# Seven-product values in the second and third batch, casts on GpSimd, sums in pieces

## The chip, the cores and the metric

The kernel runs on one core of one Trainium2 chip. The metric is the device time of one execution in microseconds; of several runs the median is given. One execution is taken by the hardware profiler, and all views of the profile are of that one. The engines are called as in the profile: PE (TensorE, matmuls), PEld (its weight loads), DVE (VectorE), ACT (ScalarE), POOL (GpSimd) and SP (SyncE, which here issues DMAs in order).

## What is computed

Attention in which a query sees only the keys of its own cluster, then a gated feed-forward block over all tokens. There are 4 batches, 8 heads, 768 tokens and 64 columns per head; 16 centroids per head; d_model 512, d_ff 1536.

```python
q_assign = argmax(einsum('bhsd,hcd->bhsc', q_n, c_n))      # k_assign alike
mask = q_assign[:, :, :, None] == k_assign[:, :, None, :]
scores = where(mask, scale * q @ k.T, -1e9)
attn = exp(scores - max) / sum
x = (attn @ v) laid out as [3072, 512]
gate = 1 / (1 + exp(-(x @ w_gate)))
out = (gate * (x @ w_val)) @ w_out
```

## The kernel before

**Attention** runs as 384 steps, 96 for a batch. A step is one score matmul of 128 x 384 (L1066, tile sc), its exp on ACT (L1071, es) and, two steps later, three matmuls of the weights with the values (L1089, av). PE executes in program order, and so does every other engine, so the order in which the program issues instructions is the schedule.

**Preparation** of later heads is issued at given step numbers by `at(step, ...)`. For a pair of heads `pair_prep` (L1624) splits keys and queries into a high and a low half-precision part: a cast on DVE (L1631, tile hl) and a subtract on POOL (L1632), four of each for a pair. Then SP issues a DMA transpose (L412, tile T); the logits against the centroids (L436, lg) and the cluster pick on DVE (L451 to L471: lgs, mx, oh) follow. `v_cast` (L324, POOL) and `v_sum` (L332 to L339, DVE) prepare the values.

**Feed-forward.** The attention result of a batch is transposed into xTb. Its feed-forward work is put into a queue of atoms and is run during the next batch's 96 steps: each step adds a number of nanoseconds to a credit (ns20 to ns33 in the table of numbers, for quarters of a batch), and atoms are taken while it lasts. For a token half (blk, 384 tokens) and each of 12 column blocks (fc) of 128, `ffn_atoms` (L517) issues a gate group (4 matmuls 128 x 384, L532, and tanh on ACT, L538, tile th) and a value group (4 matmuls, L548, and one DVE instruction, L553, that forms (th + 1) * v into hT). The factor from the sigmoid in terms of tanh is folded elsewhere.

**Output.** `product_out` (L917) multiplies a pair of token blocks, or two pairs at once, by w_out in seven products (two 2x2 block matrices with seven half-size products in place of eight). It uses two PSUM banks, x and y, in turn; each product ends with an add on DVE into ob (L941) that frees its bank for the next but one. The operand sums come from `Sums.make` (L892, L909 to L915; 128 x 768). In the second and third batch the pair (0, 1) is done alone, its atoms alternating with gate and value groups of the second token half (`aside`); then (3, 2) and (4, 5) are done together.

The last batch has no attention behind it. `closing` does its gates and values in seven products too, over 2x2 blocks of (token half, pair of column blocks, half of the 512 rows). For this, `fin_weights` (L608) makes differences of weights and `fin_tokens` (L622) sums of tokens, on DVE.

**Buffers.** th has 3, the ring of PSUM banks for scores, gates and values 4, the output banks 2, hl 4, T 8, the raw keys and queries 3 each.

## Time and profile before

| | |
|---|---|
| Median of 3 runs | 319.14 us (319.08 to 319.54) |
| The profiled execution's own time | 319.12 us |
| Its span, first to last instruction | 317.3 us |
| Mean granted clock of PE | 1.00 |
| Matmuls and their weight loads | 3492 each |
| HBM traffic | 28.34 MB read, 6.29 MB written |

The span is what the profile's views cover; 1.8 us of the execution lie outside it. Busy times of PE overlap, since matmuls are pipelined: how long one holds the engine is seen in the distance from its start to the next start. A row of the timeline is start, duration, engine, line, operation, out<-in, partitions x columns and a count of joined instructions. A row of groups is line, engine, operation, tiles, shapes, count, busy us, mean ns of one, then idle time before and what ended it. A row of windows is the stretch, its length, and busy us (with counts) of PE, PEld, DVE, ACT and POOL, the clock, the DMA share and GB/s.

### The profile page before, as it was taken

Reading aid. Unit: us, or ns where it says so; the run is one execution under the profiler, and the core shown is the slowest. Engines: PE = TensorE matmul, PEld = TensorE weight load, DVE = VectorE, ACT = ScalarE, POOL = GpSimd, SP = SyncE. Lnnn points to the kernel's source line nnn. Section 1 sums busy time; section 2 is a strip of 40 time slices with the busy share of each in tenths; the row PEclk is TensorE's granted clock in tenths of the full one; section 3 lists DMA queues with packets and bytes.
Section 4 is the critical chain, followed back from the end, with each engine's and each line's share of the span. In section 5 each row is a group of like instructions: output and inputs, shape, how many; then the busy total and the mean of one; then the engine's idle time right before and its main releaser. Section 6 shows DMA issues by size and latency. Waiting matters only on the chain.

```text
span 317.3 us, 9228 instructions
## 1 busy us (share of the span) xinstructions
PE 310.0 (98%) x3492; PEld 218.8 (69%) x3492; DVE 238.6 (75%) x623; ACT 244.9 (77%) x555; POOL 120.9 (38%) x157
## 2 busy tenths in 40 slices
PE   7899999999999999999999999999999999999995
PEld 4688766766666666666777678766677678656685
DVE  5899756778688777686788688776888776678983
ACT  6688998797899887877776876777877887588621
POOL 5888454244434275423234333424212111026600
PEclk9999999999999999999999999999999999999999
DMA  7999998639848988976676455882506130300014
GB/s 196 379 259 169 271 164 143 176 83 264 242 100 163 204 221 136 199 217 161 106 193 153 151 118 134 248 153 53 112 2 76 55 27 14 145 1 3 0 35 165
DMA packets 77996, 45.16 MB, mean 142 GB/s; under 512 B 56896, under 2 KB 75520, under 8 KB 77952
## 3 DMA queue, kind: packets, MB, share of 16 engines
q1 hardware_dynamic: 73840, 39.66, 51.3%
q0 software_dynamic: 3680, 4.72, 9.1%
q8 instruction: 27, 0.44, 0.6%
q10 hardware_dynamic: 432, 0.20, 0.2%
q14 instruction: 17, 0.14, 0.1%
HBM read 28.34 MB, written 6.29 MB: 109 GB/s over the span
## 4 chain that ended last, share of the span: by engine, by line
PE 93%; DMA 2%; DVE 1%; POOL 1%; SPq 1%; issue 0%; ACT 0%; DVEq 0%
PE sc L1066 19%; PE g L532 15%; PE v L548 15%; PE av L1089 11%; PE o L994 9%; PE o L865 5%; PE lg L436 2%; PE o L699 2%; PE o_end L802 2%; PE av L699 2%; DMA kraw<-in_k_dram 2%; PE v L628 2%; PE y L699 2%; PE o L802 1%; PE av L802 1%; PE z L699 1%
## 5 line engine op out<-in xcount | busy, mean ns | idle before, releaser
L1071 ACT ACTIVATE es<-sc 128x384 f16<-128x384 f32 x384 | 174.1, 492 | 38.5 <-PE sc L1066 29.8
L1066 PE MATMUL sc<-T 128*128 128x384 f16 x384 | 117.3, 325 | 0.7 <-DVE T L1396 0.4
L1089 PEld LDWEIGHTS <-es 128*128 128x128 f16 x1152 | 81.3, 98 | 35.1 <-ACT es L1071 0.2
L1089 PE MATMUL av<-va,es 128*128 128x65 f16 x1152 | 97.6, 194 | 0.0
L553 DVE SCALAR_TENSOR_TENSOR hT<-th,v 128x384 f16<-128x384 f32 x72 | 39.8, 553 | 33.8 <-PE av L1089 29.6
L377 POOL TENSOR_TENSOR xp<-t,rec 128x384 f16<-128x384 f32 (+1 forms) x30 | 21.8, 726 | 97.3 <-DVE rec L374 49.2
L548 PE MATMUL v<-xTb,wv 128*128 128x384 f16 x288 | 58.5, 326 | 0.1
L532 PE MATMUL g<-xTb,wg 128*128 128x384 f16 x288 | 58.5, 326 | 0.0
L538 ACT ACTIVATE th<-g 128x384 f32<-128x384 f32 x72 | 35.4, 492 | 8.3 <-PE g L532 6.3
L1066 PEld LDWEIGHTS <-T 128*128 128x128 f16 x384 | 37.0, 96 | 1.2 <-DVE T L1396 0.7
L548 PEld LDWEIGHTS <-wv 128*128 128x128 f16 x288 | 28.0, 97 | 13.9 <-issue 0.3
L532 PEld LDWEIGHTS <-wg 128*128 128x128 f16 x288 | 27.9, 97 | 13.9
L1632 POOL TENSOR_TENSOR hl<-kraw,hl 128x384 f16<-128x384 f32 x22 | 20.2, 920 | 40.6 <-DVE hl L1631 25.9
L1632 POOL TENSOR_TENSOR hl<-qraw,hl 128x384 f16<-128x384 f32 x22 | 21.1, 961 | 11.1 <-DVE hl L1631 11.1
L865 PE MATMUL o<-wo,hT 128*128 128x512 f16 x72 | 19.9, 379 | 0.0
L372 DVE TENSOR_TENSOR t<-av,sv 128x390 f32<-128x390 f32 (+1 forms) x30 | 14.4, 480 | 7.1 <-PE av L1089 5.3
L941 DVE TENSOR_TENSOR ob<-o,ob 128x256 f32<-128x256 f32 (+1 forms) x28 | 15.0, 549 | 4.7 <-PE o L994 3.2
L708 POOL TENSOR_TENSOR hT<-T 128x384 f16<-128x384 f32 x12 | 11.8, 1001 | 16.2 <-DVE T L657 15.6
L994 PE MATMUL o<-wo,hT 128*128 128x256 f16 x108 | 16.8, 272 | 0.0
L994 PEld LDWEIGHTS <-sum 128*128 128x128 f16 x144 | 14.0, 97 | 3.3
L451 DVE TENSOR_REDUCE lgs<-lg 128x192 f32<-128x384 f32 x23 | 12.7, 551 | 3.0 <-PE lg L436 2.9
L324 POOL CAST va<-vraw 128x768 f16<-128x768 f32 x15 | 13.1, 873 | 2.4 <-DMA vraw<-in_v_dram 2.4
(225 smaller groups left out, 470.2 us busy)
## 6 DMA issues: line engine op xcount, KB each, us to landing
vraw<-in_v_dram SPq DMA_DIRECT2D x15, 384.0 KB, 4.9
kraw<-in_k_dram SPq DMA_DIRECT2D x14, 384.0 KB, 4.2
qraw<-in_q_dram SPq DMA_DIRECT2D x12, 384.0 KB, 4.1
out_dram<-ob SPq DMA_DIRECT2D x17, 256.0 KB, 2.2
wg<-in_moe_w_gate_dram POOLq DMA_DIRECT2D x2, 768.0 KB, 9.2
wv<-in_moe_w_val_dram POOLq DMA_DIRECT2D x2, 768.0 KB, 10.4
wo<-in_moe_w_out_dram POOLq DMA_DIRECT2D x2, 768.0 KB, 9.3
T<-ohT SPq DMA_DIRECT2D x44, 24.0 KB, 1.9
```

What stands on the lines that cost most here:

```text
L377: (eng or POOL).tensor_tensor(x, t[:, 0:nq, 0:64], bcast(rec[:, 0:nq], 64), ALU.mult)
L532: PE.matmul(out=g[:, 0:n], lhsT=wg[fc // WQ][:, dc, fc % WQ, :], rhs=xT[:, dc, t0 : t0 + n], start=(dc == 0), stop=(dc == NDC - 1),)
L538: ACT.activation(th[:, 0:n], g[:, 0:n], AF.Tanh)
L548: PE.matmul(out=w[:, 0:n], lhsT=wv[fc // WQ][:, dc, fc % WQ, :], rhs=xT[:, dc, t0 : t0 + n], start=(dc == 0), stop=(dc == NDC - 1),)
L553: DVE.scalar_tensor_tensor(HB[b, blk][:, fc, 0:n], st[0][:, 0:n], 1.0, w[:, 0:n], ALU.add, ALU.mult)
L699: PE.matmul(out=o, lhsT=l, rhs=r, start=start and d == 0, stop=stop and d == 1, skip_group_check=True,)
L865: PE.matmul(out=o, lhsT=HB[b, blk][:, fc, bass.ts(t, 128)], rhs=wo[fc // WON][:, fc % WON, :], start=(fc == 0), stop=(fc == NFC - 1),)
L994: PE.matmul(out=st[z][:, e], lhsT=a[:, c, :], rhs=rhs[:, c, :], start=start and c + e == 0, stop=c == HF - 1, skip_group_check=True,)
L1066: PE.matmul(out=sc.rearrange("p (c t) -> p c t", t=128), lhsT=s["k"], rhs=s["q"], start=True, stop=True,)
L1071: ACT.activation(es, sc, AF.Exp, scale=SCALE)
L1089: PE.matmul(out=av[:, a0 + s["c0"] + i, :], lhsT=s["es"][:, bass.ts(i, 128)], rhs=VA[b, p][:, e, s["j"], :], start=(first and i == 0 and a ...
L1632: POOL.tensor_tensor(hl[:, :, 64:128], r, hl[:, :, 0:64], ALU.subtract)
```

## The change

For the second and third batch (b = 1, 2) a new function `middle` takes the place of `ffn_atoms`.

- Column blocks 0 to 5 of the first token half stay plain. Blocks 6 to 11 are taken in three pairs (6, 8, 10) for both token halves: each pair's values come from seven products of two matmuls each (`quarter`), where plain groups take sixteen matmuls. Gates stay plain. Plain gate and value groups of blocks 0 to 5 of the second half stand between the products.
- A product's results pass through PSUM banks x, y (the output banks) and z (the ring). ACT copies three of them to SBUF (c1, c12, c22), DVE adds others to those; (th + 1) * v is then formed by DVE or, for two of the four results of a pair, by POOL (L966), for which POOL (L948, even blocks) or ACT (L950, odd blocks) adds 1 to th.
- The sums for the output come in pieces of two column blocks between the products, and the output products are regrouped: pairs (0, 2) and (1, 3) together, then (4, 5) alone, with nothing between its atoms but attention.
- `fin_tokens` runs for b = 1, 2 too; the differences of weights move to other steps (fwg, fwv), the third sum of tokens of the last batch too (fs3).
- For b = 2, 3 the casts of keys and queries (32 in all, "pc") and the first add of `v_sum` (8, "pv") go from DVE to POOL; these casts and their subtracts are issued 1.5 steps earlier.
- Buffers: hl 4 to 2 (with 2 more up to the second batch), T 8 to 7 (and one for the last head of the first batch), raw keys and queries 3 to 2 (and one for a pair of heads in each of the first two batches). The freed room holds the differences of weights, sums of tokens and copies. The room in `closing` is assigned in another order. The credit per step (ns20 to ns33) is about 2% lower, 5% at the end.

Everything up to about step 128 stays as it was on PE, ACT and SP, and PE's order up to about step 206. Over the program PE has 12 matmuls and 12 weight loads fewer, ACT 24 instructions more, DVE 9 fewer and POOL 58 more.

```diff
@@ the table of numbers
-    -1, "b1lv1": 0.5, "b1lv2": 0.5, "b1lv3": 1.5, "ns02": 490, "ns03": 490, "ns20": 500,
-    "ns21": 491, "ns22": 481, "ns23": 410, "ns30": 443, "ns31": 443, "ns32": 443, "ns33": 423,
+    -1, "b1lv1": 0.5, "b1lv2": 0.5, "b1lv3": 1.5, "ns02": 490, "ns03": 490, "ns20": 491,
+    "ns21": 481, "ns22": 472, "ns23": 402, "ns30": 434, "ns31": 434, "ns32": 434, "ns33": 400,
-    "b3p0vs": -30, "b3p0vu": -28, "b3p0vt": -9, "b3p1lg0": -32, "b3p1pk0": -32, "fwg": [327, 327, 331, 331.5, 332, 341, 341, 344],
-    "fwv": [354, 356, 357, 359, 364, 366, 370, 371], "b3p2pk1": -28.5, "END": 0,
+    "b3p0vs": -30, "b3p0vu": -28, "b3p0vt": -9, "b3p1lg0": -32, "b3p1pk0": -32, "fwg": [353, 355, 357, 359, 361, 363, 365, 367],
+    "fwv": [172, 177, 182, 187, 369, 371, 373, 375], "b3p2pk1": -28.5, "fs3": 30, "pc": (2, 3), "pv": (2, 3), "b2p0sp00": -59.0,
...
@@ v_sum
-            eng.tensor_tensor(st["a"], r[:, :, 0:3], r[:, :, 3:6], ALU.add)
+            (POOL if b in SCHED["pv"] else eng).tensor_tensor(st["a"], r[:, :, 0:3], r[:, :, 3:6], ALU.add)
@@ the token sums and the seven products
...
+    def fin_tokens(xT, t, b=B - 1):
...
+    def quarter(xT, w, f, o, k, start, stop):
+
+        i, qn = f // WQ, f % WQ // 2 - (FC0 // 2 if f < WQ else 0)
+        T_ = lambda t, d: (fin["T", w, i, t][d] if isinstance(fin["T", w, i, t], list) else fin["T", w, i, t][:, d])[:, qn]
+        W_ = lambda k_, j, d: (wg, wv)[w][i][:, 2 * k_ + d, (f + j) % WQ, :]
+        A_ = lambda i_, k_, d: xT[:, 2 * k_ + d, 384 * (1 - i_) : 384 * (2 - i_)]
+        S_ = lambda t, d: fin["S", t][:, d]
+        for d in range(2):
+            l, r = {
+                1: lambda: (W_(0, 0, d), A_(0, 0, d)), 2: lambda: (W_(1, 0, d), A_(0, 1, d)),
+                3: lambda: (W_(1, 1, d), S_(4, d)), 4: lambda: (T_(4, d), A_(1, 1, d)),
+                5: lambda: (T_(1, d), S_(1, d)), 6: lambda: (T_(2, d), S_(2, d)),
+                7: lambda: (T_(3, d), S_(3, d)),
+            }[k]()
+            PE.matmul(
+                out=o, lhsT=l, rhs=r, start=start and d == 0, stop=stop and d == 1,
+                skip_group_check=True,
+            )
@@ new
+    MID = (1, 2)
+
+    def middle(xT, b):
+
+        gcost, pcost = NDC * 384 / 2.4 + 3, 2 * 163.0
+        c12, c22, c1 = home("c")
+        ths = {}
+        ON_POOL = ((0, 1), (1, 1))
+
+        def gate(fc, blk):
+            def f():
+                if (fc, blk) == (0, 0):
+                    for i in range(2):
+                        HB[b, i] = htp.tile([128, NFC, 384], HP, name="hT")
+                need(*(("x", b, p, 3 * blk + c) for p in range(NP) for c in range(3)))
+                g = fin_group(xT, 0, fc, blk)
+                th = ths[fc, blk] = thp.tile([128, 384], FP, name="th")
+                ACT.activation(th, g, AF.Tanh)
+                if fc >= HF and (fc % 2, blk) == (0, 1):
+                    POOL.tensor_scalar(th, th, 1.0, None, ALU.add)
+                if fc >= HF and (fc % 2, blk) == (1, 1):
+                    ACT.activation(th, th, AF.Copy, bias=1.0)
+
+            return (gcost, f)
+
+        def from_bank(fc, blk, v):
+            DVE.scalar_tensor_tensor(HB[b, blk][:, fc], ths[fc, blk], 1.0, v, ALU.add, ALU.mult)
+
+        def val(fc, blk):
+            return (gcost, lambda: from_bank(fc, blk, fin_group(xT, 1, fc, blk)))
+
+        def value(f, k):
+            st = units.setdefault(f, {})
+
+            def out(c, z, j, blk):
+                DVE.tensor_tensor(c, z, c, ALU.add)
+                if (j, blk) in ON_POOL:
+                    POOL.tensor_tensor(HB[b, blk][:, f + j], c, ths[f + j, blk], ALU.mult)
+                else:
+                    from_bank(f + j, blk, c)
+
+            def g():
+                if k == 1:
+                    taken["pair"] = True
+                    st["x"] = out_bank()[:, 0:384]
+                if k == 5:
+                    st["y"] = out_bank()[:, 0:384]
+                o = bank(512, name="z")[:, 0:384] if k == 2 else st["y" if k in (5, 3) else "x"]
+                quarter(xT, 1, f, o, k, k in (1, 2, 5), True)
+                if k in (1, 6, 7):
+                    ACT.activation({1: c1, 6: c12, 7: c22}[k], o, AF.Copy)
+                if k == 2:
+                    out(c1, o, 0, 1)
+                if k == 7:
+                    out(c22, st["y"], 1, 0)
+                if k == 3:
+                    out(c12, o, 1, 1)
+                if k == 4:
+                    from_bank(f, 0, o)
+
+            return (pcost, g)
+
+        units = {}
+        sm = {x: Sums(b, *x) for x in ((0, 2), (1, 3), (4, 5))}
+        m0, ma, mb = sm.values()
+        part = lambda m, i, *c: (0.0, lambda: m.make(i, *c))
+        G, V = (lambda f, j, i: gate(f + j, 1 - i)), value
+        for m, i in ((m0, 1), (ma, 1), (m0, 3), (ma, 3), (m0, 2), (ma, 2)):
+            m.of[i] = sump.tile([128, HF, 128], HP, tag="sum", name="sum")
+        early = [x for fc in range(HF) for x in (gate(fc, 0), val(fc, 0))] + [part(m0, 3)]
+        late = [(0.0, lambda: fin_tokens(xT, 4, b))]
+        sums = []
+        for f in (6, 8, 10):
+            p, n = f - 6, f - 5
+            w = [V(f, 1), G(f, 0, 0), V(f, 2), V(f, 5), gate(p, 1), V(f, 6), val(p, 1), G(f, 1, 1)]
+            w += [V(f, 7), G(f, 0, 1), gate(n, 1), V(f, 4), val(n, 1), G(f, 1, 0), V(f, 3)]
+            for k, x in zip((2, 5, 8, 10), sums):
+                w.insert(k + sums.index(x), x)
+            late += w
+            sums = [part(m, i, p, n + 1) for i in (1, 2) for m in (m0, ma)]
+        outs = product_out(b, [m0, ma])
+        n = 2 * HF // SCHED.get("og", 3)
+        for k, x in (
+            (5 * n, part(mb, 2)), (4 * n + n // 2, part(mb, 3)), (4 * n, part(mb, 1)), (n + 2, part(ma, 3)),
+            (n + 1, sums[3]), (n, sums[2]), (2, sums[1]), (1, sums[0]),
+        ):
+            outs.insert(k, x)
+        late += outs + product_out(b, [mb])
+        return early, late
@@ pair_prep
             if side == 0:
-                st["hl", e] = hlp.tile([128, 12, 128], HP, tag="hl", name="hl")
+                st["hl", e] = new_hl(b)
             hl, r = st["hl", e][:, 6 * side : 6 * side + 6], RAW["kq"[side], b, p][:, e]
-            DVE.tensor_copy(hl[:, :, 0:64], r)
+            (POOL if b in SCHED["pc"] else DVE).tensor_copy(hl[:, :, 0:64], r)
             POOL.tensor_tensor(hl[:, :, 64:128], r, hl[:, :, 0:64], ALU.subtract)
@@ the main loop
+    for k, s_ in enumerate(SCHED["fwv"]):
+        at(s_, lambda k=k: fin_weights(1, 1 - k // 4, 1 + k % 4))
...
+                if b in MID:
+                    at(u + lag, lambda xT=xT, b=b, i=i: middle_block(xT, b, i))
+                    if i == 0:
+                        for t in (1, 2, 3):
+                            at(u + 7 + 2 * t, lambda xT=xT, b=b, t=t: fin_tokens(xT, t, b))
+                    continue
                 at(u + lag, lambda xT=xT, b=b, a=c0 + z * w, n=z: ffn_block(xT, 128 * a, 128 * n, b))
```

**POOL in the first value pair of the second batch.** The names: hl the split keys or queries, xp the normalised attention result, va the values. Before:

```order
L377 TENSOR_TENSOR xp_3299<-t_3474,rec_3476 128x6x64
L1632 TENSOR_TENSOR hl_3503<-kraw_3236,hl_3503 128x6x64
L1632 TENSOR_TENSOR hl_3503<-qraw_3244,hl_3503 128x6x64
L1632 TENSOR_TENSOR hl_3621<-kraw_3236,hl_3621 128x6x64
L377 TENSOR_TENSOR xp_3299<-t_3667,rec_3669 128x6x64
L1632 TENSOR_TENSOR hl_3621<-qraw_3244,hl_3621 128x6x64
L324 CAST va0_167<-vraw_2837 128x12x64
L377 TENSOR_TENSOR xp_3678<-t_3864,rec_3866 128x6x64
```

Now:

```order
L1775 CAST hl_3508<-kraw_3262 128x6x64
L1776 TENSOR_TENSOR hl_3508<-kraw_3262,hl_3508 128x6x64
L948 TENSOR_SCALAR th_3553<-th_3553 128x384
L1775 CAST hl_3508<-qraw_3270 128x6x64
L1776 TENSOR_TENSOR hl_3508<-qraw_3270,hl_3508 128x6x64
L966 TENSOR_TENSOR hT_3285<-misc_132,th_3553 128x384
L1775 CAST hl_3631<-kraw_3262 128x6x64
L1776 TENSOR_TENSOR hl_3631<-kraw_3262,hl_3631 128x6x64
L399 TENSOR_TENSOR xp_3328<-t_3699,rec_3701 128x6x64
L1775 CAST hl_3631<-qraw_3270 128x6x64
L1776 TENSOR_TENSOR hl_3631<-qraw_3270,hl_3631 128x6x64
L354 TENSOR_TENSOR va3_3760<-vraw_2843 128x384
```

The casts (L1775) stand in front of their subtracts, and the multiplies (L966) and the add to th (L948) stand between them.

**DVE at the output product that is done alone**, before (third batch, pair (0, 1)); ob<-o (L941) is an end add, L553 a value group's result, L608 differences of weights:

```order
L941 TENSOR_TENSOR ob_5343<-o_5342,ob_5343 128x256
L915 TENSOR_TENSOR sum_5286<-hT_4772,sum_5286 128x768
L553 SCALAR_TENSOR_TENSOR hT_5297<-th_5521,v_5547 128x384
L372 TENSOR_TENSOR t_5556<-av_5392,sv_5207 128x390
L374 RECIPROCAL rec_5558<-t_5556 128x6
L941 TENSOR_TENSOR ob_5343<-o_5341,ob_5343 128x256
L348 TENSOR_SCALAR sv_5576<-vs_ps_5574 128x130
L553 SCALAR_TENSOR_TENSOR hT_5297<-th_5587,v_5608 128x384
L332 TENSOR_TENSOR va3_5617<-vraw_4805 128x384
L608 TENSOR_TENSOR kraw_5406<-wg0_153,kraw_5406 128x2x256
L608 TENSOR_TENSOR kraw_5407<-wg0_153 128x2x256
L941 TENSOR_TENSOR ob_5343<-o_5342,ob_5343 128x256 x2
```

Now (second batch, pair (4, 5); end adds are L1078, the cluster pick L461 to L481, L370 and L394 belong to attention):

```order
L1052 TENSOR_TENSOR sum_4529<-hT_3285,sum_4529 128x768
L370 TENSOR_SCALAR sv_4692<-vs_ps_4690 128x130
L461 TENSOR_REDUCE lgs_4717<-lg_4704 128x192
L472 TENSOR_REDUCE mx_4719<-lgs_4717 128x12
L474 TENSOR_TENSOR oh0_143<-lgs_4717,mx_4719 128x6x16 x2
L481 TENSOR_SCALAR oh0_143<-oh0_143 128x6x16
L1078 TENSOR_TENSOR ob_4622<-o_4621,ob_4622 128x256
L1078 TENSOR_TENSOR ob_4622<-o_4620,ob_4622 128x256 x2
L394 TENSOR_TENSOR t_4762<-av_4673,sv_4502 128x195
L396 RECIPROCAL rec_4764<-t_4762 128x3
L1078 TENSOR_TENSOR ob_4622<-o_4621,ob_4622 128x256
L461 TENSOR_REDUCE lgs_4803<-lg_4767 128x192
```

The end adds of the lone product now have the pick and attention's work between them, and no result of a value group.

**DVE in the first value pair of the second batch**, now; misc and hl2 hold the copies c1, c12, c22, and L955 forms (th + 1) * v:

```order
L964 TENSOR_TENSOR misc_132<-z_3565,misc_132 128x384
L461 TENSOR_REDUCE lgs_3624<-lg_3597 128x192
L472 TENSOR_REDUCE mx_3626<-lgs_3624 128x12
L474 TENSOR_TENSOR oh0_143<-lgs_3624,mx_3626 128x6x16 x2
L481 TENSOR_SCALAR oh0_143<-oh0_143 128x6x16
L955 SCALAR_TENSOR_TENSOR hT_3285<-th_3592,v_3634 128x384
L964 TENSOR_TENSOR hl2_3218<-o_3577,hl2_3218 128x384
L955 SCALAR_TENSOR_TENSOR hT_3284<-th_3652,hl2_3218 128x384
L394 TENSOR_TENSOR t_3699<-av_3525,sv_3334 128x390
L396 RECIPROCAL rec_3701<-t_3699 128x6
L370 TENSOR_SCALAR sv_3716<-vs_ps_3714 128x130
L955 SCALAR_TENSOR_TENSOR hT_3284<-th_3680,o_3537 128x384
```

The three adds onto copies (L964, two of them here) and the results that come from banks (v, o) or from a copy (hl2) stand here, where before there was one L553 for each value group.

179 lines of the change are left out of this document (100 added, 79 removed), and 1 row of the table SCHED.

## The prediction

> **What bounds the kernel now.** I read the page's busy times first, then its chain of waits, then the windows by stage, then the timeline step by step.
>
> ```profile
> PE 310.0 (98%) x3492; PEld 218.8 (69%) x3492; DVE 238.6 (75%) x623; ACT 244.9 (77%) x555; POOL 120.9 (38%) x157
> PE 93%; DMA 2%; DVE 1%; POOL 1%; SPq 1%; issue 0%; ACT 0%; DVEq 0%
> ```
>
> TensorE (PE) is busy for 310.0 of 317.3 us, and 93% of the chain that ended last lies on it. The busy columns of the windows below (us: PE, PEld, DVE, ACT, POOL) show the second batch's feed-forward (128 to 200), the third's (200 to 273, with the change of stage at 247) and the closing.
>
> ```profile
> 128.00:200.00 72.00, 71.93 (x802) 51.66 (x801) 54.63 (x143) 55.03 (x124) 24.23 (x29) 1.00 0.68 164
> 200.00:247.00 47.00, 47.00 (x505) 32.49 (x504) 36.26 (x94) 37.55 (x86) 12.78 (x16) 1.00 0.51 98
> 247.00:273.00 26.00, 26.00 (x279) 19.73 (x276) 19.22 (x42) 19.79 (x42) 3.71 (x6) 1.00 0.23 49
> 273.00:315.00 42.00, 41.00 (x299) 28.53 (x296) 32.11 (x68) 25.00 (x58) 11.80 (x12) 1.00 0.14 50
> ```
>
> In the two stages that the change touches PE is busy for 144.93 of 145 us at a granted clock of 1.00, so matmuls taken out there come off the end unless a new wait is put in. Busy durations of matmuls overlap, so what one of them costs is read from starts, in one step of the third batch:
>
> ```profile
> 201.04 0.32 PE L1066 MATMUL sc<-T 128*128 128x384 f16 x1
> 201.20 0.26 PE L1089 MATMUL av<-va,es 128*128 128x65 f16 x3
> 201.29 0.32 PE L1066 MATMUL sc<-T 128*128 128x384 f16 x1
> 201.46 0.81 PE L548 MATMUL v<-xTb,wv 128*128 128x384 f16 x4
> 201.53 0.87 ACT L1071 ACTIVATE es<-sc 128x384 f16<-128x384 f32 x2
> 202.10 0.25 PE L1089 MATMUL av<-va,es 128*128 128x65 f16 x3
> 202.19 0.33 PE L1066 MATMUL sc<-T 128*128 128x384 f16 x1
> ```
>
> Four value matmuls (L548) hold PE from 201.46 to 202.10, 0.16 us each. A step without feed-forward work takes 0.25 us (201.04 to 201.29), one with a value group 0.90 (201.29 to 202.19). Two exps (ACT) end 0.87 us after the first begins, 0.38 apart: the exps of bare steps alone would be slower than PE, and it is the feed-forward work between them that keeps PE the bound.
>
> **The change, part by part: PE.** For each of three pairs of value column blocks, 16 matmuls (two blocks, two token halves, four each) become seven products of two. That is 2 fewer for a pair, 6 for a batch, 12 for the two batches, and their weight loads go too. The output matmuls are regrouped, not reduced. 12 x 0.1625 (0.65/4, from 201.46 to 202.10 with one more digit) = **-1.95 us**. If nothing waits, that is the whole effect, and no other part can add to it.
>
> **The other engines.** The rows for what goes and comes:
>
> ```profile
> L553 DVE SCALAR_TENSOR_TENSOR hT<-th,v 128x384 f16<-128x384 f32 x72 | 39.8, 553 | 33.8 <-PE av L1089 29.6 <-PE v L548 3.6
> L1631 DVE CAST hl<-qraw 128x384 f16<-128x384 f32 x22 | 9.0, 410 | 0.0
> L1631 DVE CAST hl<-kraw 128x384 f16<-128x384 f32 x22 | 8.4, 382 | 0.0
> L332 DVE TENSOR_TENSOR va<-vraw 128x384 f32<-128x384 f32 x12 | 7.3, 611 | 0.0
> L656 DVE TENSOR_TENSOR T<-y,T 128x384 f32<-128x384 f32 x8 | 4.4, 554 | 1.1 <-ACT T L705 0.8 <-PE y L699 0.2
> L909 DVE TENSOR_TENSOR sum<-hT 128x768 f16<-128x768 f16 x7 | 4.3, 618 | 0.1
> L909 DVE TENSOR_TENSOR sum<-hT 128x256 f16<-128x256 f16 x1 | 0.3, 282 | 0.0
> L1287 POOL CAST hl<-kraw 128x384 f16<-128x384 f32 x2 | 1.0, 499 | 0.0
> L1632 POOL TENSOR_TENSOR hl<-qraw,hl 128x384 f16<-128x384 f32 x22 | 21.1, 961 | 11.1 <-DVE hl L1631 11.1
> L708 POOL TENSOR_TENSOR hT<-T 128x384 f16<-128x384 f32 x12 | 11.8, 1001 | 16.2 <-DVE T L657 15.6
> L705 ACT ACTIVATE T<-o 128x384 f32<-128x384 f32 x15 | 7.3, 490 | 3.2 <-PE o L699 2.7 <-DMA xTb<-xp 0.5
> L758 ACT ACTIVATE T<-T 128x384 f32<-128x384 f32 x15 | 7.8, 519 | 0.4 <-DVE T L656 0.4
> ```
>
> DVE loses 32 casts (32 x 0.396, the mean of 0.410 and 0.382 = 12.7), 8 first value sums (8 x 0.611 = 4.9) and 12 final multiplies (12 x 0.553 = 6.6). It gains 18 adds for the seven products (18 x 0.554 = 10.0), 8 token sums (8 x 0.618 = 4.9), and pieces of output sums: 24 more of 256 columns, 8 fewer of 768 (24 x 0.282 - 8 x 0.618 = 1.8). Net -7.5 us. POOL gains 32 casts x 0.499 = 16.0, 12 multiplies x 1.001 = 12.0, 8 first sums and 6 instructions that add 1 to a tanh. For those two it has no row: each lies between a one-operand cast (0.499) and a two-operand multiply (1.001). I take the subtract's 0.96 for the sums (two operands), 7.7, and the middle, 0.75, for the others, 4.5. Together +40 us (35 to 42): 121 becomes 161. ACT gains 18 copies x 0.490 and 6 tanh + 1 x 0.519 = +11.9 us, in stages where it now is busy for 112.4 of 145 (55.03 + 37.55 + 19.79), so 86%.
>
> None of it is on PE's path by totals. What hides it is PE itself: a value pair with the groups between it is about 14 us of PE work with 18 to 20 steps. The order of matmuls puts a gate or a plain value group between nearly any product and the next that needs its copy, so that each copy has 0.9 us or more, against 0.49 of its own and one exp ahead of it. I take 0 for these waits; without that cover each late copy would cost PE what it is late, at most about 0.5.
>
> The closest buffer is tanh's (three slots). POOL releases one after: the add on DVE (0.55), the tanh + 1 (0.75), a cast and its subtract that can stand ahead in POOL's order (0.50 + 0.96), and the multiply (1.00): 3.8 us. From the z product (value product 2) to the gate whose tanh takes that slot again PE has four groups of 0.65, three products of 0.33 and some eight steps of 0.25, 5.6 us, so 1.8 us stay. The moved casts also start the transposes on SP's queue; they are issued 1.5 steps earlier, 1.3 us at 0.90, which is more than the 0.1 us by which a POOL cast is longer, and ten steps lie between a transpose and the logits that first read it. The sixteen weight differences (L608) only change their steps; they stand in none of the places below. I take 0 here too; if POOL is late, the second rival prices it.
>
> **The lone output product.** Where I do expect waits is the product of tokens 4 and 5. Before, a lone product's pieces stood among gate and value groups; now it follows the two-pair product alone, back to back, on the two banks x and y. Its phase is six matmuls of 256 columns; three of them make a step 0.58 long:
>
> ```profile
> 187.95 0.33 PE L1066 MATMUL sc<-T 128*128 128x384 f16 x1
> 188.12 0.49 PE L994 MATMUL o<-wo,hT 128*128 128x256 f16 x3
> 188.53 0.33 PE L1066 MATMUL sc<-T 128*128 128x384 f16 x1
> ```
>
> So a phase takes about 1.1 us under attention, and 0.65 (six of 0.109, (0.58 - 0.25)/3) where attention has run out. A bank comes back when DVE's end add is done:
>
> ```profile
> L941 DVE TENSOR_TENSOR ob<-o,ob 128x256 f32<-128x256 f32 x14 | 5.6, 410 | 0.0
> 196.85 0.55 DVE L451 TENSOR_REDUCE lgs<-lg 128x192 f32<-128x384 f32 x1
> 197.43 0.35 DVE L462 TENSOR_REDUCE mx<-lgs 128x12 f32<-128x192 f32 x1
> 197.82 0.42 DVE L464 TENSOR_TENSOR oh<-lgs,mx 128x96 f16<-128x96 f32 x2
> 198.28 0.19 DVE L471 TENSOR_SCALAR oh<-oh 128x96 f16<-128x96 f16 x1
> 198.38 0.68 DVE L941 TENSOR_TENSOR ob<-o,ob 128x512 f32<-128x512 f32 x1
> ```
>
> An add of 0.41 fits into a phase. In the second batch, though, a whole cluster pick stands ahead of the fourth product's end add (lgs, mx, two oh, oh: 196.85 to 198.38, 1.53 us). The add then ends 1.53 + 0.41 = 1.94 us after the logits, against a phase of 1.1 and part of another: a wait of 0 (logits early by a phase) to 0.85, with a second pick two phases later, 0 to 0.55. I take 0.45 for both, a little under the middle, since logit matmuls lengthen PE's side by over 1 us there. In the third batch the last phases run with attention gone: two token sums (2 x 0.55) and the seventh product's two adds stand ahead of the end adds that free the banks, against phases of 0.65: 0 to 1.1, taken 0.45. Behind the waiting matmuls stand the scores, hence the exps; PE waits in order, so each counts in full. Sum **+0.9 us** (0 to 2.5).
>
> 319.12 (the profiled execution, 1.8 us more than its span; the median, 319.14, is the same within 0.02) - 1.95 + 0.9 = **318.1 us**. Its own range: 317.3 to 319.0.
>
> **Rivals.** *No wait at all*: the cover of the two-pair product, which PE passed before without a stall, holds for the lone one too, and the picks' logits come early. 319.12 - 1.95 = 317.2. For it: DVE is 7.5 us lighter. Against: the back-to-back phases of 0.65 us.
>
> *POOL holds the tanh buffers* (slower). POOL's order is fixed: two casts with two subtracts, a value cast and a multiply in a row make 2 x 1.46 + 0.87 + 1.00 = 4.8 us. If the multiply falls behind such a run, the tanh after next waits, the exps behind it on ACT wait, and PE stops with full score banks. It decides from a lag of 1.8 us on. 4.8 - 1.8 = 3.0 us at worst; taken once in each of four of the six pairs, at a bit over a third of the worst, 4 x 1.1 = 4.4: 319.12 - 1.95 + 4.4 = 321.6. For it: POOL's rows are the longest here. Against: it is busy for 40.7 of the 145 us now, and for some 81 (56%) after, even if all 40 us fell there.
>
> *DVE and POOL slow each other* (no change). These rows show it:
>
> ```profile
> 185.57 0.91 POOL L1632 TENSOR_TENSOR hl<-kraw,hl 128x384 f16<-128x384 f32 x1 [3.10 <-issue]
> 185.93 0.97 DVE L909 TENSOR_TENSOR sum<-hT 128x768 f16<-128x768 f16 x1
> 186.93 0.56 DVE L911 TENSOR_TENSOR sum<-sum,hT 128x768 f16<-128x768 f16 x1
> ```
>
> A sum that began while POOL subtracted took 0.97, the next one, with POOL idle, 0.56: 0.4 us more. With POOL busy for twice as long, its sums and picks in front of the end adds grow by that. Four to five such hits in the lone products and the output sums, on top of the 0.9, make 4.5 x 0.25 (a part of each is hidden) = 1.1: 319.2. Against: most DVE work here reads one operand from PSUM, like the final multiplies with their even 0.553.
>
> The Trainium skill ("SBUF — State Buffer", "Who interferes with whom") states that a DVE instruction with two SBUF inputs contends with a GpSimd instruction that reads SBUF, and that DVE casts can take the shared port pair whole. The pair of rows above agrees, 0.97 against 0.56; by that rule alone moving casts to GpSimd cuts both ways, since DVE's own locks go with them, and the sum would move towards 319.2 only if the hits fell on the end adds.
>
> **Chances.** The forecast (some waits, 317.3 to 319.0) 0.48; no wait, 0.18; mutual slowing to no change, 0.18; POOL late, 0.16. About 0.2% (0.64 us: under 318.5, over 319.8) is what a measurement of this kernel can tell from no change. Faster: all of no wait and three quarters of the forecast, with a few in a hundred of the third: 0.18 + 0.36 + 0.03 = 0.57. Slower: POOL late, 0.14, and 0.02 of the contention: 0.16. The same: 0.27. The range for eight in ten reaches from just under no wait, 316.9, to where POOL is late by half its price, 320.6; the two ends leave out some 2 in 10, nearly all above.
>
> **What would show it.** PE's rows: 12 fewer 384-column matmuls and weight loads, spacing still 0.16. Waits of PE in the second and third batch: only at the matmuls of the lone product, on DVE's end adds, 0.9 us together; none at value products. POOL busy about 161 us, DVE about 231, ACT about 257. POOL is right if no tanh waits for a POOL multiply. I am wrong if PE's waits exceed 2 us or lie within the value pairs, if tanh rows show idle time released by POOL, or if exps become late because ACT's copies stand ahead of them, which totals can't exclude.

## The result, and the profile after

The changed kernel takes 328.53 us (median of 4 runs, 328.41 to 329.05) beside 319.11 us for the kernel before on the same chip: a ratio of 1.0298, 95% interval 1.0282 to 1.0314. It is 9.4 us slower, where 1.0 us faster was forecast.

The page of the changed kernel, its busy times and the shares of its chain of waits:

```profile
PE 312.2 (96%) x3480; PEld 219.9 (67%) x3480; DVE 247.8 (76%) x614; ACT 253.1 (77%) x579; POOL 166.5 (51%) x215
PE 74%; DVE 13%; POOL 6%; issue 3%; DMA 2%; ACT 1%; ACTq 0%; DVEq 0%; POOLq 0%
```

PE has the 12 matmuls fewer. But its share of the chain fell from 93% to 74%, and DVE and POOL together have 19% of it where they had 2%. DVE, which by count should have been 7.5 us lighter, is busy for 9.2 us more (247.8 against 238.6). The same three stretches of time as before, though by then the changed kernel is somewhat further back in its work (us busy on PE, PEld, DVE, ACT, POOL):

```profile
128.00:200.00 72.00, 68.24 (x733) 47.98 (x732) 57.98 (x127) 56.69 (x131) 47.12 (x58) 1.00 0.64 152
200.00:247.00 47.00, 44.59 (x489) 30.03 (x488) 35.67 (x86) 37.67 (x89) 25.80 (x33) 1.00 0.43 109
247.00:273.00 26.00, 24.31 (x262) 18.24 (x260) 20.25 (x46) 20.60 (x47) 7.87 (x9) 1.00 0.17 21
```

PE is idle for 7.9 of 145 us (137.14 busy), against 0.07 before, at the same clock of 1.00. DVE is still far from full over a whole stretch (113.9 of 145): the means don't show what holds PE up. The waits do. Four rows of PE's waits and one of DVE's in the changed kernel (what waited, for what, us in total, times, longest):

```profile
PE sc L1210 <- DVE hT L955: 2.7, 3, 1.2
PE o L1131 <- DVE ob L1078: 2.5, 3, 1.3
PE sc L1210 <- DVE lgs L461: 1.5, 1, 1.5
PE z L676 <- DVE lgs L461: 0.9, 1, 0.9
DVE va L360 <- POOL va L354: 6.8, 5, 2.6
```

Each row of PE here is released by DVE: scores and products wait for a bank that DVE has still to empty. And DVE itself stood for 6.8 us behind POOL's first value add.

Two kinds of lateness are seen in one stretch, the two-pair output product of the second batch. The timeline of the changed kernel, DVE and then POOL (start, duration):

```profile
180.57 1.51 DVE L1046 TENSOR_TENSOR sum<-hT 128x256 f16<-128x256 f16 x2
182.00 0.79 DVE L1048 TENSOR_TENSOR sum<-sum,hT 128x256 f16<-128x256 f16 x2
182.71 1.26 DVE L1050 TENSOR_TENSOR sum<-hT 128x768 f16<-128x768 f16 x1
183.89 0.68 DVE L1078 TENSOR_TENSOR ob<-o,ob 128x512 f32<-128x512 f32 x1
186.33 0.56 DVE L360 TENSOR_TENSOR va<-va 128x128 f32<-128x128 f32 x1 [1.76 <-POOL va L354]
...
180.10 1.00 POOL L966 TENSOR_TENSOR hT<-hl,th 128x384 f16<-128x384 f32 x1 [3.74 <-ACT es L1215]
181.05 0.87 POOL L399 TENSOR_TENSOR xp<-t,rec 128x384 f16<-128x384 f32 x1
181.88 0.56 POOL L1775 CAST hl<-kraw 128x384 f16<-128x384 f32 x1
182.52 1.04 POOL L1776 TENSOR_TENSOR hl<-kraw,hl 128x384 f16<-128x384 f32 x1
183.51 0.83 POOL L1775 CAST hl<-qraw 128x384 f16<-128x384 f32 x1
184.41 0.91 POOL L1776 TENSOR_TENSOR hl<-qraw,hl 128x384 f16<-128x384 f32 x1
185.28 1.01 POOL L354 TENSOR_TENSOR va<-vraw 128x384 f32<-128x384 f32 x1
```

POOL works without a gap from 180.10 on. Two sums of 256 columns, 0.28 us each by the row that the prediction used, take 1.51; a sum of 768 takes 1.26 in place of 0.55. The end add (L1078), whose first operand comes from PSUM, takes its usual 0.68. Then DVE waits 1.76 us for the value add, which stands seventh in POOL's queue. The rows of the same operations over the whole profile, before and after:

```profile
L464 DVE TENSOR_TENSOR oh<-lgs,mx 128x96 f16<-128x96 f32 x42 | 9.4, 266 | 0.7
L471 DVE TENSOR_SCALAR oh<-oh 128x96 f16<-128x96 f16 x22 | 4.2, 189 | 0.8
L338 DVE TENSOR_TENSOR va<-va 128x128 f32<-128x128 f32 x12 | 3.7, 309 | 0.1
```

```profile
L474 DVE TENSOR_TENSOR oh<-lgs,mx 128x96 f16<-128x96 f32 x42 | 13.9, 370 | 0.7
L481 DVE TENSOR_SCALAR oh<-oh 128x96 f16<-128x96 f16 x22 | 6.6, 300 | 0.8
L360 DVE TENSOR_TENSOR va<-va 128x128 f32<-128x128 f32 x12 | 7.8, 648 | 6.8 <-POOL va L354 6.8
L1046 DVE TENSOR_TENSOR sum<-hT 128x256 f16<-128x256 f16 x13 | 6.6, 517 | 0.0
L955 DVE SCALAR_TENSOR_TENSOR hT<-th,v 128x384 f16<-128x384 f32 x24 | 13.2, 551 | 5.9 <-PE av L1233 5.3 <-PE v L685 0.3
```

The same instructions, the same shapes: 266 became 370 ns, 189 became 300, 309 became 648. A sum of 256 columns takes 517, where the one row of before had 282. The last row, with one operand in PSUM, takes 551, against 553 before.

To see where PE lost the time, I took the distance from each matmul's start to the next and what exceeds the usual one (0.162 us for 384 columns, 0.109 for 256, 0.032 for 65), from 90 us on. Steps are counted by score matmuls. The places of the changed kernel's larger waits have rows; all of the excess, small pieces and other places too, is in the last row.

```
step, PE stands before                    before  after   e1    e5    e15
145  scores                                  -     0.39  0.39  0.39    -
177  logits of a later head                  -     0.30  0.68  0.39    -
194  scores (token sums and a pick on DVE)   -     1.12  0.72  0.72  0.69
215  scores, in the first value pair         -     0.74  0.82  0.82    -
262-272  two-pair product, second batch    0.23    2.55  0.58  0.58  2.83
283  lone product, second batch              -     1.47  1.47    -   0.82
290-295  scores, gate and value groups       -     0.26  0.26  1.27  0.61
323  value product into z                    -     1.09    -     -     -
346  scores                                  -     1.37    -     -     -
375  two-pair product, third batch           -     0.65  0.65  0.65  0.64
383  lone product, third batch               -     0.47  0.47  0.47  0.47
all from 90 us on                           3.9   15.3  10.6   9.8  11.3
```

15.3 - 3.9 = 11.4 us of new waits, less 1.95 for the 12 matmuls, is 9.45, the 9.4 again: PE's starts add up to the span, so all of the loss lies in these waits, and the table says where (the e columns are experiments, below).

### The profile page after: what moved, and what is told of

The parts are those of the page before. It is cut to its first block, busy times and chain, and to the rows that moved or that the text cites. A ratio compares the mean times of both kernels' runs of the same rounds, so it can differ in the third digit from the quotient of the medians.

```text
span 326.6 us, 9235 instructions
## 1 busy us (share of the span) xinstructions
PE 312.2 (96%) x3480; PEld 219.9 (67%) x3480; DVE 247.8 (76%) x614; ACT 253.1 (77%) x579; POOL 166.5 (51%) x215
## 4 chain that ended last, share of the span: by engine, by line
PE 74%; DVE 13%; POOL 6%; issue 3%; DMA 2%; ACT 1%; ACTq 0%; DVEq 0%; POOLq 0%
PE sc L1210 15%; PE av L1233 8%; PE g L685 8%; PE o L1131 6%; PE v L685 5%; PE o L676 4%; PE g L542 4%; PE v L558 4%; PE o L911 3%; PE o_end L848 2%; PE av L676 2%; PE lg L446 2%; PE y L676 2%; DMA T<-hl 2%; PE z L676 1%
## 5 line engine op out<-in xcount | busy, mean ns | idle before, releaser
L1210 PE MATMUL sc<-T 128*128 128x384 f16 x384 | 118.6, 326 | 5.0 <-DVE hT L955 2.7
L685 PE MATMUL g<-xTb,wg 128*128 128x384 f16 x208 | 42.4, 326 | 0.1
L1776 POOL TENSOR_TENSOR hl<-kraw,hl 128x384 f16<-128x384 f32 x22 | 21.5, 979 | 22.5 <-DVE hl L1775 21.2
L685 PEld LDWEIGHTS <-wg 128*128 128x128 f16 x208 | 20.2, 97 | 11.8 <-issue 1.6
L946 ACT ACTIVATE th<-g 128x384 f32<-128x384 f32 x48 | 23.7, 494 | 4.4 <-PE g L685 3.3
L685 PE MATMUL v<-xTb,wv 128*128 128x384 f16 x128 | 25.9, 326 | 0.0
L563 DVE SCALAR_TENSOR_TENSOR hT<-th,v 128x384 f16<-128x384 f32 x24 | 13.2, 552 | 12.7 <-PE av L1233 10.6
L558 PE MATMUL v<-xTb,wv 128*128 128x384 f16 x96 | 19.5, 326 | 0.0
L542 PE MATMUL g<-xTb,wg 128*128 128x384 f16 x96 | 19.5, 326 | 0.0
L394 DVE TENSOR_TENSOR t<-av,sv 128x390 f32<-128x390 f32 (+1 forms) x30 | 14.3, 477 | 5.2 <-PE av L1233 5.1
L955 DVE SCALAR_TENSOR_TENSOR hT<-th,v 128x384 f16<-128x384 f32 x24 | 13.2, 551 | 5.9 <-PE av L1233 5.3
L1078 DVE TENSOR_TENSOR ob<-o,ob 128x512 f32<-128x512 f32 (+1 forms) x28 | 15.0, 549 | 3.3 <-PE av L1233 1.6
L685 PEld LDWEIGHTS <-wv 128*128 128x128 f16 x128 | 12.5, 97 | 6.9 <-issue 0.2
```

Of the source, the lines that this page charges most:

```text
L542: PE.matmul(out=g[:, 0:n], lhsT=wg[fc // WQ][:, dc, fc % WQ, :], rhs=xT[:, dc, t0 : t0 + n], start=(dc == 0), stop=(dc == NDC - 1),)
L558: PE.matmul(out=w[:, 0:n], lhsT=wv[fc // WQ][:, dc, fc % WQ, :], rhs=xT[:, dc, t0 : t0 + n], start=(dc == 0), stop=(dc == NDC - 1),)
L685: PE.matmul(out=o[:, 0:384], lhsT=w[:, dc, fc % WQ, :], rhs=xT[:, dc, 384 * blk : 384 * blk + 384], start=(dc == 0), stop=(dc == NDC - 1),)
L946: ACT.activation(th, g, AF.Tanh)
L1210: PE.matmul(out=sc.rearrange("p (c t) -> p c t", t=128), lhsT=s["k"], rhs=s["q"], start=True, stop=True,)
L1776: POOL.tensor_tensor(hl[:, :, 64:128], r, hl[:, :, 0:64], ALU.subtract)
```

## The experiments

Times are medians; "over before" is against the runs of the kernel before on the same chip, with the interval of the ratio.

| Run | us | over before (ratio, 95% interval) | POOL busy | DVE busy |
|---|---|---|---|---|
| the change | 328.53 | +9.4 (1.0282 to 1.0314) | 166.5 | 247.8 |
| e1, value adds back on DVE | 323.59 | +4.3 (1.0099 to 1.0154) | 159.7 | 250.6 |
| e2, casts back on DVE | 326.40 | +7.1 (1.0189 to 1.0234) | 150.7 | 256.6 |
| e3, both back | 324.42 | +5.1 (1.0123 to 1.0174) | 144.0 | 260.9 |
| e4, moved casts and adds alone | 321.08 | +1.7 (1.0032 to 1.0072) | 144.3 | 231.7 |
| e5, e1 and two picks later | 323.09 | +3.6 (1.0094 to 1.0153) | 159.9 | 250.8 |
| e6, e1 and multiplies on DVE | 323.71 | +4.3 (1.0117 to 1.0156) | 141.8 | 252.6 |
| e7, before and idle copies on POOL | 321.97 | +2.5 (1.0062 to 1.0101) | 160.9 | 246.9 |
| e8, before and idle constants on POOL | 321.14 | +1.7 (1.0035 to 1.0071) | 160.8 | 243.8 |
| e9, e5 and DVE's side work spread | 323.00 | +3.8 (1.0090 to 1.0142) | 160.3 | 250.5 |
| e10, e9 and half the casts on DVE | 322.80 | +3.6 (1.0095 to 1.0136) | 152.5 | 255.7 |
| e11, third batch alone, nothing else moved to POOL | 320.75 | +1.4 (1.0024 to 1.0057) | 132.7 | 246.9 |
| e12, e11 and 16 casts on POOL | 320.71 | +1.4 (1.0027 to 1.0056) | 140.9 | 244.6 |
| e13, value adds' readers later | 327.26 | +7.7 (1.0213 to 1.0265) | 166.7 | 248.6 |
| e14, e1 with casts on ACT | 323.95 | +4.4 (1.0106 to 1.0167) | 143.1 | 248.2 |
| e15, POOL's work as before | 324.49 | +4.9 (1.0129 to 1.0189) | 125.6 | 262.6 |

**Taking the change apart: e1 to e4.** The theory was that POOL makes DVE late in two ways (A, DVE stands in order behind it; B, DVE's instructions are slowed); the rival (C), that the seven products' own needs are the cost. e4 also issues casts and subtracts 1.5 steps earlier, as the change does; its listing leaves that out.

```diff
-    "pc": (2, 3), "pv": (2, 3),
+    "pc": (2, 3), "pv": (),        # e1
+    "pc": (), "pv": (2, 3),        # e2
+    "pc": (), "pv": (),            # e3
```

```diff
 # e4: the kernel before, with
-            eng.tensor_tensor(st["a"], r[:, :, 0:3], r[:, :, 3:6], ALU.add)
+            (POOL if b > 1 else eng).tensor_tensor(st["a"], r[:, :, 0:3], r[:, :, 3:6], ALU.add)
-            DVE.tensor_copy(hl[:, :, 0:64], r)
+            (POOL if b > 1 else DVE).tensor_copy(hl[:, :, 0:64], r)
```

> The changed kernel with one part undone: the first add of the value sums (8 of them) is back on DVE, the casts stay on POOL. Theory A (DVE, in order, stands still behind POOL's late value add: 6.3 us of DVE waiting on 4 occasions in the changed kernel, most of PE's waits come from it): 328.5 falls to 322 to 325, DVE's waits for POOL go to nearly 0. Theory B (POOL, busier, slows each DVE instruction with two operands in SBUF): 327 to 328. Theory C (the seven products' own use of banks and buffers): 328.5 as it is.

323.59, A's figure: 4.9 us of the 9.4 go with eight instructions moved back. In the table of waits the places 323 and 346 are empty, and 262-272 falls from 2.55 to 0.58: those are the places at which DVE stood behind the value add.

> The changed kernel with the 32 casts back on DVE; the value adds stay on POOL. Theory A: POOL's queue is 17.6 us shorter, the value add is late less often, 321 to 325. Theory B: POOL is busy for 17.6 us less, half of the slowing goes: 323 to 326. Theory C: 328.5 or more, since DVE has 12.7 us more to do.

326.40, 0.4 above B's figure, 1.4 above A's and below C's: none of the three.

> The changed kernel with casts and value adds both back on DVE: the seven products, the regrouped output and the moved weight differences alone. A and B together hold: 318 to 320, PE's waits at 1 to 2 us. Theory C: 324 or more, with PE waiting at value products and at the lone output product.

324.42, C's figure. C has a share that my theory had not: with casts and value adds where they were, the rest of the change still costs 5.1 us over the kernel before. That rest is more than the seven products: the output products are regrouped, their sums come in pieces, and POOL keeps its 12 multiplies and 6 additions of 1. With the value adds on DVE, the casts on POOL even help a little (e1 is 0.8 us below e3); with the value adds on POOL they hurt (328.53 against 326.40).

> The kernel before, with nothing but the moved casts, value adds and the 1.5 earlier steps. A and B: slower by themselves, 321 to 327, with DVE waiting for POOL's value add. Theory C, or an effect only in company (POOL's queue gets long only with the multiplies of the seven products in it): 319 to 320.

321.08, the lower end of A and B: the moves alone cost 1.7 us, 7.7 less than the change. They get dear in company.

**Is it standing, or slowing? e13.** One pair of numbers moves the two DVE instructions that read POOL's add seven steps further back:

```diff
-    "b2vu": -17,    "b3p0vu": -28,
+    "b2vu": -10,    "b3p0vu": -21,
```

> The changed kernel with one number altered: DVE's second and third value add (which read POOL's first) are issued 7 steps later. POOL does as much as in the changed kernel (328.5). If DVE standing in order behind POOL's add is the cost: as e1, 323.3 to 324.5, DVE's waits for POOL near 0. If POOL's share of the adds slows DVE otherwise: 326 to 328.

327.26: the rows of DVE waiting for POOL are gone from its waits, yet only 1.3 of e1's 4.9 us came back. Mere standing doesn't explain e1. PE's waits at 323 and 346 (2.46 us together) are gone here as they are in e1, so those two were the standing; but others came, 0.71 at 191, 0.91 at 308 and 0.39 at 329 among them. The same adds at their new place run beside POOL (191.83, 192.78), and the end adds of the two-pair product start late behind them:

```profile
191.83 0.92 DVE L360 TENSOR_TENSOR va<-va 128x128 f32<-128x128 f32 x1
192.78 0.48 DVE L361 TENSOR_TENSOR vs<-va,va 128x128 f16<-128x128 f32 x1
193.17 1.27 DVE L1078 TENSOR_TENSOR ob<-o,ob 128x512 f32<-128x512 f32 x2
```

A wait of 1.43 us of PE stands there now (step 272), where the change had none; e2, e3 and e15, which have the casts on DVE, have 1.32 to 1.37 at the same place. How the other 3.6 us of e1 divide between POOL's 8 us less of reading and where the adds land was not separated.

**The slowing by itself: e7 and e8.** The kernel before, with idle work on POOL behind 32 subtracts, which nothing waits for:

```diff
             POOL.tensor_tensor(hl[:, :, 64:128], r, hl[:, :, 0:64], ALU.subtract)
+            if b > 1:
+                ...
+                for _ in range(3):
+                    POOL.tensor_copy(idle, r[:, 0:4])        # e7
+                for _ in range(4):
+                    POOL.memset(idle, 0.0)                   # e8
```

> The kernel before, with idle work on POOL that nobody waits for: behind each of the 32 subtracts of the third and fourth batch's keys and queries three copies of 256 columns from SBUF into an unused tile, about 40 us in all, as much as the change adds. Theory of slowing: DVE's busy time grows by 8 us or more though its work is the same (oh, the multiply after it, the sums), and the time by 0.5 to 3 us. Rival (only queue order counts): DVE's busy time grows by under 2 us, and the time by what is queued behind the copies, under 1 us.

321.97, and DVE busy 246.9 against 238.6 with the same 623 instructions: 8.3 us of pure stretching, as the theory of slowing had it. Of the 2.5 us, PE's longest wait is for a late transpose, 1.4 us at the logits of step 177, since the copies hold up the next subtract; so queue order counts too.

> The same with POOL writing constants instead (four of 256 columns, about 40 us, nothing read from SBUF). If it is POOL's reading that slows DVE: DVE's busy time as before within 2 us and 319.1 to 319.6. If any work of POOL does, or POOL's queue: as the copies.

321.14, with DVE at 243.8: neither of the two outcomes. The constants delay POOL's other work (step 177 waits 1.2 us here too), and this reading work then runs beside DVE's picks. The single instructions tell it apart. Two stretches of e8's timeline, DVE and POOL:

```profile
202.60 0.43 DVE L464 TENSOR_TENSOR oh<-lgs,mx 128x96 f16<-128x96 f32 x2
203.06 0.22 DVE L471 TENSOR_SCALAR oh<-oh 128x96 f16<-128x96 f16 x1
...
202.55 1.05 POOL L1636 MEMSET c<- 128x256 f16 x3
```

```profile
114.66 1.05 DVE L464 TENSOR_TENSOR oh<-lgs,mx 128x96 f16<-128x96 f32 x2
115.75 1.03 DVE L471 TENSOR_SCALAR oh<-oh 128x96 f16<-128x96 f16 x1
...
114.72 0.89 POOL L324 CAST va<-vraw 128x768 f16<-128x768 f32 x1
115.57 0.92 POOL L1632 TENSOR_TENSOR hl<-qraw,hl 128x384 f16<-128x384 f32 x1
```

Beside constants the pair of comparisons takes 0.43, as alone; beside a cast and a subtract 1.05. Over e8's profile from 90 to 285 us, each instruction sorted by what POOL did meanwhile (mean ns, count):

```
                     POOL idle   constants only   POOL reads SBUF
oh<-lgs,mx            254 (21)      250 (7)          620 (7)
sum<-hT 768           553 (6)       552 (2)          788 (4)
oh<-oh, one operand   187 (12)      300 (5)         1029 (1)
lgs<-lg, from PSUM    552 (8)       547 (7)          538 (2)
hT<-th,v, v in PSUM   551 (17)      552 (7)          553 (33)
```

What slows an instruction with two operands in SBUF is POOL's reading, not its being busy; the single-operand f16 multiply is held up by writing too (five cases); an instruction with an operand in PSUM by neither. The Trainium skill ("SBUF — State Buffer", "Who interferes with whom") states this rule: two SBUF inputs contend with a GpSimd instruction that reads, not with one that only writes, and casts and tensor_scalar in a two-port mode contend as a whole. These rows agree, 250 beside constants and 620 beside reads.

**The lone product: e5.**

```diff
-    "b3p1lg0": -32, "b3p1pk0": -32,
+    "b3p1lg0": -26, "b3p1pk0": -26, "b3p1lg1": -23, "b3p1pk1": -23,
```

> The value adds back on DVE (as in e1, 323.6), and the two cluster picks that fall into the second batch's lone output product issued after it (logits and pick of the second pair of heads of the last batch, from steps 280 and 283 to 286 and 289). Theory: PE's wait of 1.47 us ahead of the fifth product there is the pick in front of the end add on DVE: it goes, 322.0 to 322.6. Rival: the wait is DVE's backlog in general (sums, attention), and comes back at the next end add: 323.2 to 323.8.

323.09, between the two figures, 0.1 from the rival's. The wait of 1.47 at step 283 is gone, as the theory had it, but 1.0 of it is back at steps 290 to 295, where the moved picks now hold up gate and value groups (0.26 became 1.27). Here is the place in the changed kernel, DVE, POOL and PE, the change's own profile:

```profile
201.22 0.54 DVE L461 TENSOR_REDUCE lgs<-lg 128x192 f32<-128x384 f32 x1
201.80 0.35 DVE L472 TENSOR_REDUCE mx<-lgs 128x12 f32<-128x192 f32 x1
202.18 0.43 DVE L474 TENSOR_TENSOR oh<-lgs,mx 128x96 f16<-128x96 f32 x2
202.64 0.78 DVE L481 TENSOR_SCALAR oh<-oh 128x96 f16<-128x96 f16 x1
203.34 1.07 DVE L1078 TENSOR_TENSOR ob<-o,ob 128x256 f32<-128x256 f32 x3
...
202.39 0.99 POOL L1776 TENSOR_TENSOR hl<-qraw,hl 128x384 f16<-128x384 f32 x1
...
203.80 0.49 PE L1131 MATMUL o<-wo,sum 128*128 128x256 f16 x3 [1.30 <-DVE ob L1078]
```

The pick is in front of the end adds, as forecast; its last instruction takes 0.78 instead of 0.19 beside a subtract. A sum in front of the pick was late too (0.90 for 0.55 at 200.20).

**Where DVE's work goes: e6, e9, e10, e14, e15.** e6 sets `ON_POOL = ()` and leaves out the additions of 1, on the base of e1. e9 moves side work of e5 (fwg to 318-351, fwv to 140-170 and 343-354, token sums to steps +15, 19, 23); e10 is e9 with `"pc": (3,)`. e14 is e1 with the casts by `ACT.copy`; e15 is e3 and e6 together.

> The value adds back on DVE, and the two results of a pair that POOL multiplied formed by DVE as the others are; the 6 additions of 1 on POOL and 6 on ACT fall away. POOL loses some 19 us, DVE gains 12 instructions of 0.55 = 6.6 us by count. Theory of slowing (DVE's operations with two SBUF operands are stretched by POOL's work): DVE's busy time rises by less than 6.6 and the waits in the pairs go down, 322.5 to 323.5. Rival (DVE's own load is what makes it late): 324 to 326.

323.71, between the two figures: no change against e1. DVE's busy time rose by 2.0 for 6.6 us of added work, so 4.6 us of stretching went with POOL's 18; the wait at step 215 went, and others came. The theory's first half held, its time did not.

> As e5 (323.1), with DVE's side work moved away from the stretches in which DVE has no room left (steps 188 to 199, 248 to 271 and 356 to 379, where it is busy for 0.92 to 1.00 of the time in e5): differences of value weights from steps 172-187 and 369-375 to 140-170 and 343-354, of gate weights from 353-367 to 318-351, token sums of the two batches from steps +9, 11, 13 to +15, 19, 23. Theory (DVE full in single stretches, and PE waits there): the waits at steps 194, 375 and some of 177 go, 1.2 to 1.8 us, 321.3 to 322.0. Rival (the waits are single late instructions, picks and queues): 322.8 to 323.4.

323.00: the waits at 194 and 375 went as forecast (0.72 and 0.65), and 0.54 at 323 and 0.81 at 346 came, where the differences are now. The rival's figure.

> As e9, with the third batch's 16 casts back on DVE (only the fourth batch's stay on POOL). If the slowing by POOL is what costs between steps 140 and 220 (waits at 145, 177, 215): 0.5 to 1.5 us less than e9. If DVE's own load counts more, as e3 against e1 suggests (0.8 us more with all casts on DVE): 0.3 to 1 us more than e9.

322.80, the same as e9 within the spread of each (322.35 to 323.36 and 322.69 to 323.44). Neither direction.

> As e1 (323.6), with the 32 casts on ACT, so that neither DVE nor POOL has them. If DVE's lateness, from load or from slowing, is the cost of the rest: 320.5 to 322.5, and it would be the fastest with both batches. If ACT, with 12 us more, makes the exps late: 324 or more.

323.95, no better than e1: DVE's busy time fell only to 248.2. Of the long waits 1.14 stays at 283 and 0.65 at 375; the others broke up into many of 0.2 to 0.6, three short kinds of them for ACT.

> The seven products in both batches with nothing of it on POOL: value adds, casts and all multiplies on DVE, no addition of 1 on POOL or ACT. POOL as in the kernel before (some 121 us). If POOL's slowing is the rest of the cost: DVE's two-operand rows are as in the kernel before and the time is 320 to 322. If DVE's load in single stretches is: 324 or more, as e3 (324.4).

324.49, the second theory's figure. The engines' row of its page:

```profile
PE 311.1 (96%) x3480; PEld 219.3 (68%) x3480; DVE 262.6 (81%) x666; ACT 250.5 (78%) x573; POOL 125.6 (39%) x157
```

Groups of DVE in e15: the comparisons, the multiply after them, the first value add, the sums of 256 columns:

```profile
L474 DVE TENSOR_TENSOR oh<-lgs,mx 128x96 f16<-128x96 f32 x42 | 9.4, 266 | 0.7
L481 DVE TENSOR_SCALAR oh<-oh 128x96 f16<-128x96 f16 x22 | 4.2, 189 | 0.8
L354 DVE TENSOR_TENSOR va<-vraw 128x384 f32<-128x384 f32 x12 | 9.2, 767 | 0.0
L1042 DVE TENSOR_TENSOR sum<-hT 128x256 f16<-128x256 f16 x13 | 5.9, 466 | 0.0
L1044 DVE TENSOR_TENSOR sum<-sum,hT 128x256 f16<-128x256 f16 x13 | 5.7, 449 | 0.0
```

The picks are as fast as before the change, 266 and 189 ns. The slowing is not gone, though: the first value add takes 767 ns, where it had 611, and the sums of 256 columns 466 and 449, where a row of before had 282. PE still waits 11.3 us, 2.8 of it in the two-pair product of the second batch and 0.8 in the lone one. DVE is full there: between steps 248 and 271 it was busy for 0.89 to 0.99 of the time in e15 and 0.96 to 1.00 in e5, where the kernel before had 0.61 to 0.98 (busy time cut off at the next start, in pieces of four steps).

What filled it can be read from the traces, by setting each instruction against the median of its form where POOL was idle. For DVE's instructions of steps 248 to 271:

```
                      alone they add up to    they took longer by
kernel before               15.16 us                0.34 us
the change                  15.94                   3.54
e15                         17.65                   2.97
```

So in e15 both are up, the load by 2.5 us and the slowing by 2.6, although POOL does no more than in the kernel before: DVE has more two-operand work beside it. The run doesn't part load from slowing, and the condition of its first theory, two-operand rows as before, was not met.

**One batch alone: e11 and e12.** `MID = (2,)`, value adds on DVE, differences spread, credits of the second batch as before.

> The seven products in the third batch alone (the second as before), value adds and casts all on DVE, weight differences spread as in e9: 6 matmuls fewer, -0.98 us. If a batch of seven products needs more DVE than the stretch has, whatever POOL does: its waits (2 to 3 us in the third batch of e9) exceed that, 319.8 to 321.2. If POOL's work was what made DVE late: 318.2 to 319.0, faster than before.

320.75.

> As e11, with the last batch's 16 casts on POOL. DVE has 6.3 us less to do by count. DVE's load as the cause: 0.3 to 1 us less than e11. POOL's slowing as the cause: 0.3 to 1 us more.

320.71. A batch of seven products saves 6 matmuls, 0.98 us, and cost 1.4 over before in both arrangements, so neither direction of e12 came. The first forecast of e11 held, not cleanly: 1.05 us of its waits are a late transpose at step 177, far ahead of the third batch's products, which e12 hasn't. In e12 the waits at steps 308 to 346 (0.27, 0.45, 0.21 and 0.81) alone exceed what is saved. None of the fifteen runs beats the kernel before, so there is no version to recommend over it.

## Why the prediction was wrong

- *12 matmuls fewer, -1.95 us.* Right: 3480 for 3492, and the balance of 11.4 us of waits closes with it.
- *Waits at the lone product, +0.9 us.* The mechanism was right, its size not: 1.47 in the second batch (taken 0.45, bound 0.85 with a pick of 1.53 and an add of 0.41), 0.47 in the third (taken 0.45). The pick took 2.1 us (201.22 to 203.34) beside POOL. e5 shows that it was this pick.
- *"None of it is on PE's path by totals" and the zeros that rest on it.* This is the step that failed. The other waits, some 9.5 us, lie at places that were given 0: the two-pair product (2.55 and 0.65), the scores at 194 and 215, the value product at 323, the scores at 346. In e1 4.4 of these are gone, where DVE stood behind the value add (323, 346 and 2.0 at 262-272). DVE's mean (110.1 of 145 us before) was read as room. But PE has two output banks and a ring of four, so DVE may be late by about a phase (1.1 us in the prediction's rows) and no more; in the two-pair product of the changed kernel DVE was full for a whole stretch, 0.96 to 1.00 of steps 248 to 271 but for 260 to 263 (0.60), where it stood. Occupancy by stretches of four steps was what the argument needed, and the readers of what was moved.
- *DVE 7.5 us lighter.* It is 9.2 heavier, 16.7 off: the counts were right within one (10 fewer by the prediction's items, 623 to 614 by the profile), the durations were not. Against each form's median with POOL idle, DVE's instructions ran 24.1 us longer in the changed kernel and 9.0 in the kernel before, all of it in instructions that shared time with one of POOL: 15.1 of the 16.7. In the kernel before, 34 of 36 comparisons of picks ran while POOL did nothing, which is why their row read 266; in the changed kernel 19 of 36. Durations were taken from rows that held only for the old neighbours.
- *POOL +40 us, ACT +11.9.* 45.6 and 8.2 came. The value add took 1.016 and the addition of 1 to tanh 1.186, above both bounds that the nearest rows had given (0.499 and 1.001). ACT's new rows took what was priced (0.49 to 0.52 each).
- *The rival "POOL holds the tanh buffers".* No tanh waited for POOL. POOL was late, but the one that stood behind it was DVE: eight value adds whose readers on DVE come two steps later. I counted these adds as 8 x 0.96 of busy time and did not ask who reads them; e1 shows that they were worth 4.9 us; with the standing removed in e13, 1.3 came back net of what the moved readers cost at their new places.
- *The rival "DVE and POOL slow each other".* The right mechanism with the right row for it (0.97 against 0.56), with far too few hits: 4 to 5 of 0.25 were assumed, 15.1 us of stretching were measured. What it costs PE by itself was not separated; in e7 8.3 us of stretching and a late transpose together cost 2.5.
- *Transposes "0 here too".* PE waited 0.30 at the logits of step 177 in the change, 0.52 in e4, where the moves stand alone. That a late POOL queue does this is seen in e7 and e8 (1.4 and 1.2); that it is the whole of it in the change is not shown, since e3, with the casts on DVE, has 0.67.

That the waits come back elsewhere when one is taken away (e5, e9, e13) is shown, and so is that DVE is full where the two-pair product waits. How e1's remaining 4.3 us divide between DVE's load and its slowing stays open: e6 and e15 exchange one for the other at about the same time, and e14, which takes the casts from both engines, gains nothing. Not varied by themselves were the regrouping of the output products with their sums in pieces, the smaller buffers and the lower credit; 4.8 of e15's 11.3 us of waits lie in the output products (2.83, 0.82, 0.64 and 0.47).

## What to carry to other kernels

An engine that empties PSUM banks for the bounding engine has to be on time within a phase, so its room is read in windows as short as the buffers are deep, not from its share of a stage. When work goes to another engine, ask for each result who reads it and how soon, in both queues. And a duration from a row holds for the neighbours that it had: before POOL gets 45 us more, look at how often DVE's two-operand instructions ran beside it, and what they took when they did.
